# Moving the projection of a turn to the end of its odd unit, with three filler matmuls after each even unit, in a decode attention kernel bound by its loads

## The chip, the cores and the metric

One NeuronCore of a Trainium2 chip runs the whole kernel. The metric is device time in microseconds; the text quotes medians of several executions. The profile's span is about 2 us shorter than the device time of the same execution (443.6 against 445.62 in the profiled run of before), so I compare spans with spans and times with times. Ratios are the mean time of one kernel's runs over the mean of the other's in the same rounds, so they are not quite the ratio of the medians that stand beside them.

## The reference

Two attention layers, A and B, for one new token each, with batch 4, 32 query heads, 8 key/value heads, head size 128; B attends to the last 2048 of 8192 positions only:

```python
q = (x @ wq).reshape(B, 1, 32, 128).transpose(0, 2, 1, 3)
k = repeat(k_cache, 4, axis=1); v = repeat(v_cache, 4, axis=1)   # B: [:, :, Sk - W:, :], W = 2048
p = softmax(einsum("bhqd,bhkd->bhqk", q, k) * 128 ** -0.5)
o = einsum("bhqk,bhkd->bhqd", p, v)
out = o.transpose(0, 2, 1, 3).reshape(B, 1, 32 * 128) @ wo       # A and B concatenated
```

Nearly all of the bytes are the caches, bf16: 184.56 MB are read in all.

## The kernel before

The work is cut into 20 units, 0 to 19: four of B and sixteen of A. One unit is 4 MB of K and 4 MB of V (128 tiles each). Two units make a turn, and TensorE's program is one loop over ten turns, so every turn has the same instructions in the same order. In unit `u` TensorE transposes K tiles (T), multiplies them with the queries (S), sums the weights of the unit before (SM), and multiplies the weights of the unit before with its V (PV):

```python
LA = 3
for k in range(NJ + LA):               # NJ = 16
    if k < NJ:
        TOK.append(("T", k))
    elif k == NJ:
        TOK.append(("SM",))
    else:
        TOK.append(("PV", pc))
        pc += 1
    if k >= LA:
        TOK.append(("S", k - LA))
while pc < NC:                         # NC = 8
    TOK.append(("PV", pc))
    pc += 1
AFTER = {("S", 2): ("OT",), ("S", 5): ("OL",), ("S", 8): ("OPJ",)}
```

So the last two S of a unit stand behind the first two PV. OPJ is the projection of a piece of heads whose attention is done, eight matmuls of 512 columns. It comes after S 8 of the even unit (the flag in the code that says `odd` is true for even `u`):

```python
def fn(pe):
    for i in range(C):                 # C = 8
        ins = pe.matmul(out=bk[0:Bn, 0:D], lhsT=OL[:, i // REP, i % REP, :], rhs=Wo_sb[:, i // REP, i % REP, :],
                        start=(i == 0), stop=(i == C - 1))
    return ins
op("pe", fn, waits=[("E", ol_idx[tn]), ("wo", tn) if tn in pieces else None, bankfree(idx)], inc=("T", idx))
```

Its weights, Wo, are 1 MB for each of the turns 3 to 9, in one tile without a second buffer. All big loads are issued in one order from one queue. K of unit u may be issued when the T of unit u-2 are done, V of unit u-1 when the PV of unit u-3 are done, and Wo of a turn when the projection of the turn before is done:

```python
for u in range(1, NU + 1):             # NU = 20
    if u < NU:
        kv_load("K", u)
    kv_load("V", u - 1)
    tn = (u + 1) // 2
    if u % 2 == 1 and tn in pieces:
        ... op("sp", dma(Wo_sb, src), waits=[("T", opj_idx[tn - 1])], inc=("wo", tn))
```

After the loop comes a tail outside of it: PV of unit 19, a seed from the sums so far, and the last projection with its own tile Wl (1 MB), which is loaded last. V of unit 19 comes in four pieces.

## Time and profile before

| what | value |
|---|---|
| device time, median of 3 runs | 444.65 us (444.62 to 445.03) |
| span of the profile | 443.6 us |
| read from HBM | 184.56 MB, mean 416 GB/s |
| main DMA queue | 98.0% of 16 engines' span |
| TensorE busy | 81% |

These are rows of the page of the kernel before: the clock granted to TensorE, the busy share of the DMA engines and their rate in 40 slices of the span, then the main queue with its packets, MB and share of 16 engines' time, and one line of the list of waits (who waited for whom: us in total, times, longest).

```profile
PEclk9999999999999799789969995999799889968999
DMA  8999999999999999999999999999999999999992
GB/s 332 429 417 421 419 417 421 421 447 406 445 411 449 431 428 429 440 428 428 425 425 434 425 432 432 440 412 442 431 425 425 434 435 431 427 434 415 437 401 73
...
q1 hardware_dynamic: 13088, 184.56, 98.0%
...
PE KT L258 <- DMA K_sb<-in_A_k_cache_dram: 50.6, 8, 7.9
```

The reader should see that the DMA never rests between the first and the last slice, and that TensorE waits for it. Only the last slice (73 GB/s) has room: about 9 us from the end of the bulk of the loads to the end of the kernel.

That tail begins with K of unit 18. These lines are from the timeline of TensorE; the columns are start, us, engine, line, operation, out<-in, shapes, count, and in brackets the idle time before it and what ended it. KT, OT, SA and SB are output tiles of TensorE; KT also serves for the projection and for the last PV. ACT is ScalarE, which computes the exp of the softmax.

```profile
396.74 3.68 PE L258 MATMUL KT<-identf,K_sb 128*128 128x128 f32 x16 [7.94 <-DMA K_sb<-in_A_k_cache_dram]
...
407.54 1.89 PE L370 MATMUL KT<-Wo_sb,OL 128*4 128x512 bf16 x8
...
416.88 1.95 PE L258 MATMUL KT<-identf,K_sb 128*128 128x128 f32 x16
...
427.74 0.63 PE L307 MATMUL OT<-PT,V_sb 128*128 128x64 bf16 x16
...
429.07 2.96 PE L307 MATMUL OT<-PT,V_sb 128*128 128x64 bf16 x96
433.39 1.98 PE L307 MATMUL KT<-PT,V_sb 128*128 128x64 bf16 x64 [1.36 <-ACT PT L448]
```

Unit 18 starts at 396.74, when its K has landed, with the clock at half (16 transposes in 3.68 us; at 416.88 the same 16 take 1.95). The projection of turn 9 is at 407.54. PV of unit 18 runs from 427.74. Then TensorE stands 1.36 us for the last exp, and the PV of unit 19 starts at 433.39.

The last loads, from the timeline of the issuing queue, and the landing of the 4 MB of V of unit 18 (the last line is from the list of DMA issues for the window around 389 us: count, KB, us from issue to landing):

```profile
366.14 0.38 SPq L549 DMA_DIRECT2D Wo_sb<-in_A_wo_dram  x1
368.81 0.33 SPq L549 DMA_DIRECT2D K_sb<-in_A_k_cache_dram  x1
...
383.89 0.80 SPq L549 DMA_DIRECT2D K_sb<-in_A_k_cache_dram  x2
388.89 0.33 SPq L549 DMA_DIRECT2D V_sb<-in_A_v_cache_dram  x1
...
V_sb<-in_A_v_cache_dram SPq DMA_DIRECT2D x1, 4096.0 KB, 37.0
```

Wo of turn 9 goes ahead of K of unit 18; V of unit 18, issued at 388.89, lands at 388.89 + 37.0 = 425.9. That is only 1.8 us before TensorE comes to use it at 427.74.

### The profile page before, as it was taken

The page shows a single profiled execution, that of the slowest core. Times are in us where ns is not written, and L with a number is a line of the kernel's source. Part 1 is how long each engine was busy: PE and PEld are TensorE (multiplying, and loading weights), DVE is VectorE, ACT ScalarE, POOL GpSimd, SP SyncE. Part 2 cuts the span into 40 slices and gives each one's busy share as a digit, 9 for nine tenths or more (in the row PEclk, how much of TensorE's full clock was granted, in tenths as well). Part 3 has the DMA queues.
Part 4 walks back from the last instruction along what each step waited for, and adds up shares of the span by engine and source line. Part 5 has one row for each costly group of instructions (what it writes and reads, how often), then busy time and mean ns, then how long its engine had stood idle before and what let it go on. Part 6 is the DMA issues. An engine that isn't in the chain of part 4 may idle for free.

```text
span 443.6 us, 15670 instructions
## 1 busy us (share of the span) xinstructions
PE 358.4 (81%) x7282; PEld 335.3 (76%) x7282; DVE 210.0 (47%) x472; ACT 184.8 (42%) x184; POOL 21.4 (5%) x56
## 2 busy tenths in 40 slices
PE   0259898998994899399939975996799399929996
PEld 0248798898894889389938975896789389928995
DVE  0035356565463464256525651574355256515661
ACT  1005374374471437054525542562338054515550
POOL 6100000000000000000000000000000000000000
PEclk9999999999999799789969995999799889968999
DMA  8999999999999999999999999999999999999992
GB/s 332 429 417 421 419 417 421 421 447 406 445 411 449 431 428 429 440 428 428 425 425 434 425 432 432 440 412 442 431 425 425 434 435 431 427 434 415 437 401 73
DMA packets 13191, 184.78 MB, mean 416 GB/s; under 512 B 1348, under 2 KB 2424, under 8 KB 4472
## 3 DMA queue, kind: packets, MB, share of 16 engines
q1 hardware_dynamic: 13088, 184.56, 98.0%
q8 instruction: 8, 0.13, 0.1%
q14 instruction: 7, 0.06, 0.0%
q0 software_dynamic: 64, 0.02, 0.0%
q10 hardware_dynamic: 24, 0.01, 0.0%
HBM read 184.56 MB, written 0.01 MB: 416 GB/s over the span
## 4 chain that ended last, share of the span: by engine, by line
DMA 50%; PE 47%; issue 1%; SPq 1%; DVE 1%; ACT 0%
DMA K_sb<-in_A_k_cache_dram 43%; PE KT L258 27%; DMA K_sb<-in_B_k_cache_dram 7%; PE OT L307 5%; PE SA L291 4%; PE KT L370 4%; PE SB L291 3%; PE KT L307 1%; PE SA L319 1%; SPq L549 1%; PE KT L349 0%; PE KT L331 0%; ACT PT L448 0%; PE SA L673 0%; PE KT L673 0%
## 5 line engine op out<-in xcount | busy, mean ns | idle before, releaser
L258 PE MATMUL KT<-identf,K_sb 128*128 128x128 f32 x1280 | 207.7, 297 | 57.3 <-DMA K_sb<-in_A_k_cache_dram 50.6
L267 ACT ACTIVATE KT_sb<-KT 128x1024 bf16<-128x1024 bf16 x160 | 162.4, 1023 | 145.0 <-PE KT L258 144.7
L258 PEld LDWEIGHTS KT<-identf,K_sb 128*128 128x128 f32 x1280 | 148.9, 150 | 65.4 <-DMA K_sb<-in_A_k_cache_dram 51.8
L266 DVE COPY KT_sb<-KT 128x512 int32<-128x512 int32 x160 | 110.3, 689 | 132.1 <-PE KT L258 130.9
L307 PE MATMUL OT<-PT,V_sb 128*128 128x64 bf16 x2560 | 84.4, 193 | 1.7 <-issue 1.7
L307 PEld LDWEIGHTS OT<-PT,V_sb 128*128 128x128 bf16 x2560 | 78.4, 98 | 1.9 <-issue 1.9
L291 PEld LDWEIGHTS SA<-RQc,KT_sb 128*128 128x128 bf16 x1280 | 56.1, 98 | 3.1 <-ACT KT_sb L267 0.6
L448 ACT ACTIVATE PT<-Dt 128x1024 bf16<-128x1024 f32 (+1 forms) x21 | 21.3, 1016 | 85.6 <-DVE Dt L437 85.6
L291 PE MATMUL SA<-RQc,KT_sb 128*128 128x16 bf16 x1280 | 56.2, 170 | 0.0
L291 PE MATMUL SB<-RQc,KT_sb 128*128 128x16 bf16 x1280 | 55.7, 170 | 0.0
L291 PEld LDWEIGHTS SB<-RQc,KT_sb 128*128 128x128 bf16 x1280 | 51.6, 97 | 1.1
L399 DVE TENSOR_REDUCE M<-SB 128x8 f32<-128x512 f32 (+1 forms) x20 | 13.8, 692 | 43.4 <-PE SB L291 43.4
L420 POOL PARTITION_ALL_REDUCE MB<-M1m x20 | 7.7, 387 | 392.9 <-DVE M1m L413 392.9
L370 PE MATMUL KT<-Wo_sb,OL 128*4 128x512 bf16 x80 | 18.9, 379 | 0.0
L189 PE MATMUL KT<-ident,x_sb 4*128 4x4 bf16 x8 | 0.6, 170 | 19.3 <-POOL identf L511 19.3
L189 PEld LDWEIGHTS KT<-ident,x_sb 4*128 4x128 bf16 x8 | 0.4, 112 | 19.5 <-issue 19.5
L437 DVE TENSOR_TENSOR Dt<-SA,MBm 128x512 f32<-128x512 f32 x20 | 13.8, 691 | 0.7
L399 DVE TENSOR_REDUCE M<-SA 128x8 f32<-128x512 f32 (+1 forms) x20 | 13.6, 680 | 0.0
L437 DVE TENSOR_TENSOR Dt<-SB,MBm 128x512 f32<-128x512 f32 x20 | 13.6, 680 | 0.0
L319 PE MATMUL SA<-PT,onesb 128*128 128x64 bf16 x336 | 13.2, 192 | 0.0
L370 PEld LDWEIGHTS KT<-Wo_sb,OL 128*4 128x4 bf16 x80 | 6.0, 84 | 8.1
L319 PEld LDWEIGHTS SA<-PT,onesb 128*128 128x128 bf16 x336 | 11.1, 97 | 0.0
(68 smaller groups left out, 111.8 us busy)
## 6 DMA issues: line engine op xcount, KB each, us to landing
K_sb<-in_A_k_cache_dram SPq DMA_DIRECT2D x15, 4096.0 KB, 27.9
V_sb<-in_A_v_cache_dram SPq DMA_DIRECT2D x15, 4096.0 KB, 32.6
K_sb<-in_B_k_cache_dram SPq DMA_DIRECT2D x16, 1024.0 KB, 21.7
V_sb<-in_B_v_cache_dram SPq DMA_DIRECT2D x16, 1024.0 KB, 21.6
V_sb<-in_B_wq_dram SPq DMA_DIRECT2D x1, 4096.0 KB, 12.3
V_sb<-in_A_wq_dram SPq DMA_DIRECT2D x1, 4096.0 KB, 21.6
Wo_sb<-in_B_wo_dram SPq DMA_DIRECT2D x4, 1024.0 KB, 20.1
K_sb<-in_A_k_cache_dram SPq DMA_DIRECT2D x2, 2048.0 KB, 29.7
```

The source lines that it names most:

```text
L258: ins = pe.transpose(out=bkf[:, pi * 128:(pi + 1) * 128], in_=K_sbf[:, slot, t0:t0 + 2, :].rearrange("p t d -> p (t d)"), identity=identf[ ...
L266: return e.tensor_copy(out=KT_sb.bitcast(I32)[:, tj % NKT, :], in_=bkf.bitcast(I32)[:, :])
L267: return e.activation(out=KT_sb[:, tj % NKT, :], in_=bk[:, :], func=ACTF.Copy)
L291: ins = pe.matmul(out=stb[:, t % NTH * C:(t % NTH + 2) * C], lhsT=ktv[:, pi, :, e], rhs=RQc[:, u % 2, t // TS, e, :], start=(e == 0), stop ...
L307: ins = pe.matmul(out=otb[:, s * NW:s * NW + w], lhsT=V_sb[:, slot, t, :], rhs=PT[:, slot, t * C:t * C + w], start=(j == 0), stop=(j == n ...
L319: ins = pe.matmul(out=SA[u % 2][:, s * NW:(s + 1) * NW], lhsT=onesb[:, :], rhs=PT[:, u % 2, c0:c0 + NW], start=(i == 0), stop=(i == n - 1))
L370: ins = pe.matmul(out=bk[0:Bn, 0:D], lhsT=OL[:, i // REP, i % REP, :], rhs=Wo_sb[:, i // REP, i % REP, :], start=(i == 0), stop=(i == C - 1))
L399: return dve.tensor_reduce(out=M1[:, h * n:(h + 1) * n].rearrange("p (s h) -> p s h", h=C), in_=bank[:, :].rearrange("p (s j h) -> p s h j ...
L420: return pool.partition_all_reduce(MB[:, 0:n], M1m[:, 0:n], channels=128, reduce_op=ReduceOp.max)
L437: return dve.tensor_tensor(out=Dt[:, h * NTH * C:(h + 1) * NTH * C].rearrange("p (s j h) -> p s j h", s=Sh, h=C), in0=bank[:, :].rearrange ...
L448: return act.activation(out=PT[:, u % 2, a:b], in_=Dt[:, a:b], func=ACTF.Exp, scale=scale)
L549: return e.dma_start(out=dst, in_=src)
```

## The change

The intent is to put the projection where TensorE waits anyway (before K of the next even unit), and to fill some of the wait after even units so that TensorE's clock stays up. The core of the diff:

```diff
+        def pe_filler(n):
+            bank = (jobs[-1]["bank"] + 1) % NBK
+            ...
+                for _ in range(n):
+                    ins = pe.matmul(out=KTB[bank][:, :], lhsT=ident[:, :], rhs=RQ[0]..., start=True, stop=True)   # 512 columns, nobody reads it
...
-        AFTER = {("S", 2): ("OT",), ("S", 5): ("OL",), ("S", 8): ("OPJ",)}
+        AFTER = {("S", 2): ("OT",), ("S", 5): ("OL",)}
...
+            if u % 2 == 1:
+                ev["opj"] = pe_job_OPJ(tn)          # after the last PV of the odd unit
+            else:
+                pe_filler(NFILL)                    # NFILL = 3, after the last PV of the even unit
...
-                op("pe", pe_seed)
+                op("pe", pe_seed, waits=[("ocp", NTURN - 1)])
...
-            tn = (u + 1) // 2
-            if u % 2 == 1 and tn in pieces:
+            tn = u // 2
+            if u % 2 == 0 and tn in pieces:
```

The last four lines change the order of the loads. Before: ..., Wo of turn 9, K18, V17, K19, V18. After: ..., K18, V17, Wo of turn 9, K19, V18. This has to be so, because Wo must wait for the projection before it, which is now later.

More of the change, by code (lines that the diff above doesn't have):

```diff
@@ L52, in bass_concat_heads__gqa_block_cached__sliding_block_cached__decode_kernel @@
     NBK = 4
+    NFILL = 3
     NTH = NT // 2
@@ L244, in pe_job_perm, with fn @@
             add(dict(eng="dve", fn=efn, waits=[("T", idx)], inc=("E", idx)))
+        def pe_filler(n):
+            bank = (jobs[-1]["bank"] + 1) % NBK
+            p = bank_last[bank]
+            def fn(pe):
+                ins = None
+                for _ in range(n):
+                    ins = pe.matmul(out=KTB[bank][:, :], lhsT=ident[:, :], rhs=RQ[0][:, :, :, :, :].rearrange("p b g e c -> p (b g e c)"),
+                                    start=True, stop=True)
+                return ins
+            op("pe", fn, waits=[("F", p) if jobs[p]["turn"] is not None else None])
         def pe_T(u, k):
@@ L607, in bass_concat_heads__gqa_block_cached__sliding_block_cached__decode_kernel @@
                     kind = AFTER[tok][0]
-                    anchored({"OT": pe_job_OT, "OL": pe_job_OL, "OPJ": pe_job_OPJ}[kind](tn))
+                    anchored({"OT": pe_job_OT, "OL": pe_job_OL}[kind](tn))
+            if u % 2 == 1:
+                ev["opj"] = pe_job_OPJ(tn)
+            else:
+                pe_filler(NFILL)
+                if tn:
+                    follow[opj_idx[tn - 1]] = tjob_idx[(u, 0)]
             for k in range(0, NJ, 2):
@@ L617, in bass_concat_heads__gqa_block_cached__sliding_block_cached__decode_kernel @@
                     add(d)
-                    if "opj" in d:
-                        follow[d["opj"]] = tjob_idx[(u, k + 2)]
             add(dve_max(u, 1))
@@ L631, in bass_concat_heads__gqa_block_cached__sliding_block_cached__decode_kernel @@
                 add_norm(u - 1)
+            if u % 2 == 1:
+                add(ev["opj"])
             for k in range(1, NJ, 2):
@@ L834, in emit_pe @@
                         else:
-                            assert val <= 0, (we, val)
+                            assert val <= 0 or we[0] == "F", (we, val)
                         o["w"].append((sem, val))
```

## The prediction

> **What bounds it now.** The loads. The page's DMA row is at 9 in 38 of 40 slices; the main queue is 98.0% busy, about 426 GB/s in mid-run. The Trainium skill ("DMA: Bandwidth & Descriptors", Specifications) gives a fabric ceiling of 435 GB/s; the trace agrees that little is left. TensorE follows: in the list of waits it stands 50.6 us for A's K tiles in 8 waits, nearly all just before even units (up to 7.9 us). The queue never runs dry. So only the end can get shorter: K of unit 18 releases TensorE at 396.74, and from there the chain of waits is nearly unbroken TensorE work (units 18 and 19, last softmax, PV, projection) to 443.6.
>
> **What the change does.**
> - Projection (8 matmuls, 1.82 us, in the timeline): leaves the middle of the even unit, where it delays the T and S that follow, and goes to the end of the odd unit, into the wait for the next even K.
> - Fillers: 3 matmuls of 512 columns, at 1.82/8 = 0.23 us each: 0.68 us per turn, off the chain except the set after unit 18.
> - To my mind the largest term: the 1 MB Wo load of a turn moves from before K of the even unit to after it. Every even K from unit 6 on lands 1 MB earlier, about 2.4 us (in the sum of bytes Wo9 takes 380.75 to 383.24). Odd K keeps its position; it is issued later (behind the wait for the projection), but now lands about 30 us after issue; the queue should keep over 10 us of work.
> - TensorE's wait of 7 us per turn is divided: about 2 to 3 us before even units, the rest before odd ones. Clock: it halves after waits of 7 us, and the first 16 transposes take 3.68 us instead of 1.97. The Trainium skill ("TensorE: Matmul & The Clock Gate", Part 1) puts the drop after one idle window of about 3.4 us; here the clock fell 2.5 to 4.7 us after work stopped, agreeing roughly. Shorter waits should keep most even units warm; odd units may now start cold.
>
> **On the critical path.** At the end: K18 2.4 us earlier, projection of turn 9 out of unit 18 −1.8, fillers +0.7, projection at the end of unit 19 +0.3 to +1 (it mostly fits in the 1.36 us in which TensorE waits for exp), warm unit 18 up to −2.5 (partly lost waiting for V18). TensorE could be 3 us or more earlier. But the DMA doesn't end earlier: the last V pieces land near 435.6 and the last Wl piece near 438.4; then follow one pair of matmuls, the copy and the output's transfer (2.6 us from last matmul to end). Floor about 441.4 for the span, a gain of 2.2 us.
>
> **Time:** 442.4 us (−0.5%), range 441.0 to 443.9. Faster by over 2%: 0.02; within 2%: 0.96; slower: 0.02.
>
> **What would show it.** DMA share and GB/s per slice as before; even units' waits down from 7 to under 3.5 us, odd units' up from 0.4 to 3 to 5; fewer half-clock stretches before even units; TensorE waits for VL or Wl pieces in the last 10 us; unit 18 starting near 394.3.
>
> **What would make it wrong.** The later issue of odd K draining the queue (slower); fill or projection delaying T through bank waits; the tail's DMA stragglers moving with the earlier issue of the last V (faster, to 440); even K's landing set by the slowest DMA engine, not by its place in the bytes (no gain).

## More of the kernel before

A trace is that of one execution, and executions of one kernel differ: the spans of the kernel before go from 442.1 to 444.2 us, with a mean of 443.2.

## The result, and the profile after

| | before | changed |
|---|---|---|
| median of 4 runs | 444.79 us (444.62 to 445.03) | 445.9 us (445.18 to 447.0) |
| ratio | | 1.0027, 95% interval 1.0004 to 1.0049 |
| span of the profile | 443.6 us | 444.2 us |

The change makes the kernel slower by 0.3%. It is small, but the sign is clear, and it is not the gain of 2.2 us that I had forecast. The page of the changed kernel, the same rows and waits as above:

```profile
PEclk9999999999989997997999699979998998899989
DMA  8999999999999999999999999999999999999991
GB/s 346 414 415 423 418 418 420 422 446 405 443 437 440 425 426 434 431 425 428 434 428 434 432 437 412 442 425 428 430 437 431 437 425 426 431 420 425 432 404 57
...
q1 hardware_dynamic: 13088, 184.56, 97.9%
...
PE KT L271 <- DMA K_sb<-in_A_k_cache_dram: 42.3, 13, 6.4
PE OT L320 <- DMA V_sb<-in_A_v_cache_dram: 3.5, 1, 3.5
```

The loads run as before. TensorE waits less for K (42.3 instead of 50.6 us, spread over 13 waits instead of 8). There is one new wait, 3.5 us for V, and it happens once. The timeline of TensorE shows where:

```profile
394.47 2.10 PE L271 MATMUL KT<-identf,K_sb 128*128 128x128 f32 x16 [0.32 <-DMA K_sb<-in_A_k_cache_dram]
...
411.72 1.97 PE L271 MATMUL KT<-identf,K_sb 128*128 128x128 f32 x16 [0.69 <-DMA K_sb<-in_A_k_cache_dram]
...
426.32 0.64 PE L320 MATMUL OT<-PT,V_sb 128*128 128x64 bf16 x16 [3.47 <-DMA V_sb<-in_A_v_cache_dram]
...
427.67 4.51 PE L320 MATMUL OT<-PT,V_sb 128*128 128x64 bf16 x96
432.11 1.89 PE L383 MATMUL KT<-Wo_sb,OL 128*4 128x512 bf16 x8
433.93 1.99 PE L320 MATMUL KT<-PT,V_sb 128*128 128x64 bf16 x64
```

And the last loads:

```profile
394.18 0.38 SPq L562 DMA_DIRECT2D Wo_sb<-in_A_wo_dram  x1
394.66 0.89 SPq L562 DMA_DIRECT2D K_sb<-in_A_k_cache_dram  x2
395.65 16.52 SPq L562 DMA_DIRECT2D V_sb<-in_A_v_cache_dram  x5
...
V_sb<-in_A_v_cache_dram SPq DMA_DIRECT2D x1, 4096.0 KB, 30.6
```

The first half of the plan works. Unit 18 starts 2.3 us earlier (394.47 against 396.74), with a full clock (16 transposes in 2.10 us) and without the projection. TensorE is ready for PV of unit 18 at 426.32 - 3.47 = 422.85, against 427.74 before: 4.9 us earlier. But V of unit 18 is issued at 395.65 and lands at 395.65 + 30.6 = 426.3, where it landed before (425.9). Its place in the queue is the same, so the earlier issue brings nothing: in all twelve traces of this document in which the same bytes stand ahead of it, V18 is issued between 388.9 and 395.7 and lands between 425.8 and 426.4.

One thing more stands in the traces. A load is complete when all 16 DMA engines have done their share, and the recorded completions show that 15 of them had done theirs of V18 by 423.2 us in both kernels. The last one followed at 425.9 before and at 426.3 in the changed kernel. So 2.7 to 3.0 us of the landing time belong to one late engine; without it, the wait of the changed kernel would be about 0.4 us (an estimate from these figures: 423.2 less 422.85). Why it is late was not tested.

A ledger of the start of the last PV (433.39 before, 433.93 after):

| step | us |
|---|---|
| ready for PV of unit 18 earlier (427.74 to 422.85) | -4.89 |
| new wait for V18 | +3.47 |
| PV of unit 18 slower (4.29 us from 427.74 to 432.03 before, 5.79 us from 426.32 to 432.11 after) | +1.50 |
| projection now behind it, +1.82, while the wait of 1.36 for exp goes | +0.46 |
| sum | +0.54 |

The slower PV is the clock: 96 matmuls take 4.51 us instead of 2.96. The record of the granted clock has a stretch of half speed from 427.7 to 431.2 us, so it fell 1.4 us after the work had resumed. Without this row the sum would be -0.96 us: the wait takes most of the gain, and the slow clock turns the rest into a loss. The span grew by 0.6 us, so the trace is accounted for. The medians differ by 1.1 us, and the interval of the ratio goes from 0.2 to 2.2 us, so the rest is within the spread of the runs.

### The profile page after: what moved, and what is told of

It reads as the page before. It is cut to its first block, busy times and chain, and to the rows that moved or that the text cites. A ratio compares the mean times of both kernels' runs of the same rounds, so it can differ in the third digit from the quotient of the medians.

```text
span 444.2 us, 15710 instructions
## 1 busy us (share of the span) xinstructions
PE 367.5 (83%) x7312; PEld 339.1 (76%) x7312; DVE 211.0 (48%) x472; ACT 186.3 (42%) x184; POOL 21.3 (5%) x56
## 3 DMA queue, kind: packets, MB, share of 16 engines
q1 hardware_dynamic: 13088, 184.56, 97.9%
HBM read 184.56 MB, written 0.01 MB: 416 GB/s over the span
## 4 chain that ended last, share of the span: by engine, by line
DMA 50%; PE 47%; SPq 1%; issue 1%; DVE 0%; ACT 0%
DMA K_sb<-in_A_k_cache_dram 36%; PE KT L271 23%; PE OT L320 10%; DMA K_sb<-in_B_k_cache_dram 7%; DMA V_sb<-in_A_v_cache_dram 7%; PE KT L383 4%; PE SA L304 4%; PE SB L304 4%; SPq L562 1%; PE SA L332 1%; PE KT L320 1%; PE KT L254 0%; PE SA L692 0%; PE KT L692 0%; DVE oacc L393 0%
## 5 line engine op out<-in xcount | busy, mean ns | idle before, releaser
L271 PE MATMUL KT<-identf,K_sb 128*128 128x128 f32 x1280 | 209.4, 298 | 46.8 <-DMA K_sb<-in_A_k_cache_dram 42.3
L320 PE MATMUL OT<-PT,V_sb 128*128 128x64 bf16 x2560 | 86.0, 194 | 5.1 <-DMA V_sb<-in_A_v_cache_dram 3.5
L320 PEld LDWEIGHTS OT<-PT,V_sb 128*128 128x128 bf16 x2560 | 79.9, 99 | 5.3 <-DMA V_sb<-in_A_v_cache_dram 3.6
L304 PEld LDWEIGHTS SA<-RQc,KT_sb 128*128 128x128 bf16 x1280 | 57.0, 98 | 2.4
```

The costliest lines, as they stand in the source:

```text
L271: ins = pe.transpose(out=bkf[:, pi * 128:(pi + 1) * 128], in_=K_sbf[:, slot, t0:t0 + 2, :].rearrange("p t d -> p (t d)"), identity=identf[ ...
L304: ins = pe.matmul(out=stb[:, t % NTH * C:(t % NTH + 2) * C], lhsT=ktv[:, pi, :, e], rhs=RQc[:, u % 2, t // TS, e, :], start=(e == 0), stop ...
L320: ins = pe.matmul(out=otb[:, s * NW:s * NW + w], lhsT=V_sb[:, slot, t, :], rhs=PT[:, slot, t * C:t * C + w], start=(j == 0), stop=(j == n ...
```

## The experiments

Theory T: at the end TensorE meets the landing of V18, which is fixed by the bytes ahead of it in the queue. All gains ahead of that point are lost there, and what still stands behind it (PV at whatever clock, then the projection) sets the end. "Fixed" covers the late engine as well. Rival F: the fillers' own time ate the gain. Rival Q: the wait for the projection in the load queue delays the issue of odd K and V and so slows the loads. Each run below was compared with the kernel before in the same rounds. The fragments of the timeline are of TensorE, as above, all from the last 20 us.

| run | median us (6 runs) | before, same rounds (11 runs) | ratio, 95% interval | span of profile |
|---|---|---|---|---|
| changed, without fillers | 445.54 | 444.86 | 1.0019 (1.0000 to 1.0038) | 443.6 |
| changed, projection before the PV | 443.64 | 444.86 | 0.9975 (0.9958 to 0.9992) | 441.8 |
| before, with Wo after K | 444.02 | 444.86 | 0.9991 (0.9970 to 1.0011) | 441.9 |
| before, with fillers | 445.71 | 444.86 | 1.0014 (0.9998 to 1.0029) | 444.3 |
| changed, last Wo after V18 | 443.48 | 445.31 | 0.9959 (0.9945 to 0.9972) | 441.4 |
| changed, fillers in the wait for V | 444.04 | 445.31 | 0.9971 (0.9957 to 0.9984) | 442.3 |
| projection before the PV and all S first | 443.51 | 445.31 | 0.9956 (0.9943 to 0.9969) | 442.1 |
| the same, Wl loaded before the last V | 448.47 | 445.31 | 1.0071 (1.0053 to 1.0090) | 445.6 |
| changed, again | 446.21 | 445.08 | 1.0027 (1.0007 to 1.0047) | 444.4 |
| changed, Wo loads at their old place | 444.56 | 445.08 | 0.9991 (0.9973 to 1.0009) | 442.6 |
| before, Wo after K and all S first | 443.58 | 445.08 | 0.9977 (0.9955 to 0.9999) | 441.7 |

### The fillers: taken out of the changed kernel, and added alone

```diff
-                pe_filler(NFILL)          # in the changed kernel
```

> The changed kernel without its fillers (odd-end projection and late Wo kept). Theory T (at the end TensorE stands for V of unit 18, which lands near 426.3 whatever TensorE does, and what still stands behind that wait in TensorE's order sets the end): no gain over the changed kernel, within 0.5 us of its 445.9; TensorE only stands longer for V18, some 4.2 us instead of 3.5. Rival F (the fillers' own time is what ate the gain): at least 0.7 us faster than the changed kernel. Rival Q (the later issue of odd K and V slows the loads): no change.

```profile
411.24 1.97 PE L271 MATMUL KT<-identf,K_sb 128*128 128x128 f32 x16 [1.27 <-DMA K_sb<-in_A_k_cache_dram]
...
425.84 0.64 PE L320 MATMUL OT<-PT,V_sb 128*128 128x64 bf16 x16 [3.46 <-DMA V_sb<-in_A_v_cache_dram]
...
427.37 4.24 PE L320 MATMUL OT<-PT,V_sb 128*128 128x64 bf16 x96
```

445.54 us: no clear gain over the changed kernel. The wait for V18 did not grow to 4.2 us as expected. The time of the fillers went into the wait for K of unit 19 instead, which is 1.27 us here and 0.69 us with the fillers, so TensorE comes to V18 no earlier in relation to the loads (K of unit 19 and V18 both landed 0.5 us earlier in this run). The half clock is still there.

```diff
+        def pe_filler(n):
+            ...
+            if u % 2 == 0:
+                pe_filler(NFILL)          # in the kernel before, after the even unit
```

> The kernel before with only the three fillers after each even unit. Theory T: there TensorE reaches PV of unit 18 after V18 has landed (427.7 against 425.9), so the set after unit 18 lies on the chain: +0.7 us, 445.5; elsewhere hidden in waits. Rival F: +0.7 us or more, up to 7 us if each turn's set counted. Rival Q: nothing to say.

```profile
428.41 0.63 PE L320 MATMUL OT<-PT,V_sb 128*128 128x64 bf16 x16
```

445.71 us, with the interval of the ratio reaching just below 1. In the trace PV of unit 18 starts 0.67 us later than before (427.74), which is one set of fillers. So the nine other sets of fillers are hidden in waits, and the set after unit 18 counts in the kernel before, where TensorE neither waits for K of unit 19 nor for V18. It doesn't count in the changed kernel, where TensorE waits for both. Rival F explains the second run but not the first.

### The projection moved a little: before the PV instead of after it

```diff
+                if u % 2 == 1 and tok == ("S", NJ - 3):
+                    ev["opj"] = pe_job_OPJ(tn)
...
-            if u % 2 == 1:
-                ev["opj"] = pe_job_OPJ(tn)
-            else:
+            if u % 2 == 0:
                 pe_filler(NFILL)
```

> The changed kernel with the projection of the odd unit put just before the first PV of that unit instead of after the last. Theory T: in the last turn it fits into the wait for V18, which shrinks from 3.5 to about 1.7 us; the first PV of the last unit starts at 431 to 432 instead of 433.9; 1.8 to 3.3 us faster than the changed kernel (the upper end if the clock stays full), so 442.6 to 444. Rival F: no change against the changed kernel. Rival Q: the issue of odd K comes 6 us earlier, so the bytes of the whole queue would end earlier than 437.1; under T they end where they did.

```profile
422.73 1.89 PE L383 MATMUL KT<-Wo_sb,OL 128*4 128x512 bf16 x8
425.89 0.64 PE L320 MATMUL OT<-PT,V_sb 128*128 128x64 bf16 x16 [1.27 <-DMA V_sb<-in_A_v_cache_dram]
...
427.24 2.96 PE L320 MATMUL OT<-PT,V_sb 128*128 128x64 bf16 x96
431.53 1.98 PE L320 MATMUL KT<-PT,V_sb 128*128 128x64 bf16 x64 [1.33 <-ACT PT L461]
```

443.64 us, as theory T expects, and faster than before with an interval clear of 1. The projection lies in the wait, the wait shrinks to 1.27 us, the clock stays full (2.96 us), and the last PV starts at 431.53. The last packet of Wl in the trace ends at 438.0 us here, at 438.4 in the changed kernel, and at 438.0 in the kernel before (the 437.1 in the expectation is not an end of the loads in the trace). So the earlier issue of odd K that comes with this edit did not move the loads' end by more than these 0.4 us, and rival Q has little to explain.

### V18 moved: one load of 1 MB put behind it

```diff
-            tn = u // 2
-            if u % 2 == 0 and tn in pieces:
+            tn = 9 if u == 19 else u // 2
+            if (u % 2 == 0 and u < 18 or u == 19) and tn in pieces:
```

> The changed kernel with one load of 1 MB elsewhere: the last Wo is loaded after V of unit 18 instead of before K of unit 19. Fillers and the projection at the end of the odd unit stay. Theory T: V18 lands 2.4 us earlier (near 423.9), the wait before the PV of unit 18 shrinks from 3.5 to 1 to 2 us, too short to lower the clock; PV and projection then end near 430, and the last PV starts at 430 to 431 instead of 433.9: span 441.5 to 442.3, about 2 us faster than the changed kernel. If V18 is not the cause (rivals F, Q): no change, 445 to 446.

```profile
423.16 0.67 PE L320 MATMUL OT<-PT,V_sb 128*128 128x64 bf16 x16 [1.95 <-DMA V_sb<-in_A_v_cache_dram]
...
424.95 3.89 PE L320 MATMUL OT<-PT,V_sb 128*128 128x64 bf16 x96
428.78 1.89 PE L383 MATMUL KT<-Wo_sb,OL 128*4 128x512 bf16 x8
430.61 1.99 PE L320 MATMUL KT<-PT,V_sb 128*128 128x64 bf16 x64
...
436.65 0.27 PE L692 MATMUL SA<-Wl_sb,OT_sb 128*4 128x256 bf16 x1 [0.36 <-DMA Wl_sb<-in_A_wo_dram]
```

This is the most direct test: TensorE's program is untouched, with its fillers and its projection at the end; only the place of one load among the last ones differs. PV of unit 18 starts at 423.16 instead of 426.32, and the kernel takes 443.48 us. So the place of the last loads is the cause. The edit brings K of unit 19 1 MB forward too, and TensorE comes to V18 1.64 us earlier for that (421.21 instead of 422.85); with V18 where it was, this would only have made the wait longer. One detail of my expectation was wrong: the half clock did come (96 matmuls in 3.89 us, half speed from 423.6 to 427.0), after a wait of only 1.95 us. It cost nothing at the end: the first piece of the last V, issued at 409.88, landed 20.7 us later at 430.6, and the last PV starts at 430.61. After that TensorE runs along with the end of the loads: in the last line it is a piece of Wl that ends its wait.

### The clock: fillers in the wait for V

```diff
+                if u % 2 == 1 and tok == ("S", NJ - 3):
+                    pe_filler(14)
```

> The changed kernel with 14 more fillers (3.2 us) in every odd unit just before its first PV, so TensorE works while it would stand for V18. Theory T with the clock as a part of it: the half clock at 427.7 goes, the last 96 matmuls of PV take 2.96 us again instead of 4.51, the last PV starts 1.5 us earlier: about 1.5 us faster than the changed kernel, still with the projection on the chain: about 444.4. If the clock plays no part: no change or slower. Rival F: slower by the fillers' time.

```profile
425.97 0.64 PE L320 MATMUL OT<-PT,V_sb 128*128 128x64 bf16 x16 [0.43 <-DMA V_sb<-in_A_v_cache_dram]
...
427.32 2.96 PE L320 MATMUL OT<-PT,V_sb 128*128 128x64 bf16 x96
430.21 1.89 PE L383 MATMUL KT<-Wo_sb,OL 128*4 128x512 bf16 x8
432.03 1.99 PE L320 MATMUL KT<-PT,V_sb 128*128 128x64 bf16 x64
```

444.04 us. Adding 3.2 us of useless work to every odd unit makes the changed kernel faster. The 96 matmuls are back at 2.96 us (1.55 us less), and the last PV starts 1.90 us earlier than in the changed kernel; the other 0.35 us is V18 landing at 425.97 instead of 426.32 in this run. So the half clock is worth 1.5 us, more than the whole loss: without it the changed kernel is faster than before (0.9971). The fillers of the change itself stand after the even unit, where no such wait is on the chain.

### The two halves of the change, one at a time

First the load order alone, in the kernel before:

```diff
         if u < NU:
             kv_load("K", u)
-        kv_load("V", u - 1)
-        tn = (u + 1) // 2
-        if u % 2 == 1 and tn in pieces:
+        tn = u // 2
+        if u % 2 == 0 and tn in pieces:
             ...                            # load Wo of turn tn
+        kv_load("V", u - 1)
```

> The kernel before with one thing of the change: Wo of a turn is loaded after K of its even unit instead of before. Theory T: K of unit 18 lands about 2.4 us earlier (394.3), TensorE reaches the PV of unit 18 at about 425.3 and stands under 1.5 us for V18 (426); no projection follows, so the last PV starts at about 431 instead of 433.4: 1.5 to 2.4 us faster than before, 442.4 to 443.3. Rival F: the full 2.4 us. Rival Q: the same as T. If even K is not earlier, my account of the order of bytes is wrong: 444.8.

```profile
426.05 0.64 PE L307 MATMUL OT<-PT,V_sb 128*128 128x64 bf16 x16 [0.84 <-DMA V_sb<-in_A_v_cache_dram]
...
431.69 1.98 PE L307 MATMUL KT<-PT,V_sb 128*128 128x64 bf16 x64 [1.33 <-ACT PT L448]
```

In the trace it is as expected: unit 18 starts at 394.27, the wait for V18 is 0.84 us, the last PV starts at 431.69 instead of 433.39, the span is 441.9. In time it is a miss: the median of 444.02 is above my range, and the ratio 0.9991 is not clear of 1. Two of its six runs were at 445.4 and 445.9, with a lower mean clock (0.946 and 0.942, against 0.950 to 0.961 in the others). Their traces were not kept; that a half clock fell into the tail in them is likely, but not shown.

Then the projection alone, with the Wo loads where they were. This gives a wrong result, since the loads go to spare tiles:

```diff
+        Wx = [sb("Wx%d" % i, [128, 2, REP, D], BF16) for i in range(2)]
...
-            tn = u // 2
-            if u % 2 == 0 and tn in pieces:
+            tn = (u + 1) // 2
+            if u % 2 == 1 and tn in pieces:
-                ... dma(Wo_sb, src), waits=[("T", opj_idx[tn - 1])]
+                ... dma(Wx[tn % 2], src), waits=[("T", opj_idx[tn - 2])]
```

> The changed kernel (projection at the end of the odd unit, fillers) with the Wo loads' place in the queue as in the kernel before. That place is only free of races if the loads go to two spare tiles that nobody reads, so the result is wrong on purpose; bytes and instructions are the same, and the issue of odd K and V no longer stands behind the projection. Theory T: even K lands where it did (unit 18 from 396.7), TensorE reaches the PV of unit 18 near 426.6, after V18: no wait above 0.5 us, no half clock in the tail; PV then projection end near 432.6, the last PV from there: 0.4 to 0.9 us faster than before, thus about 1.5 us faster than the changed kernel. Each half of the change alone gains then, and only together they lose. If the projection's place alone is the loss, it is slower than before here too (445.5 or more).

```profile
426.33 0.63 PE L321 MATMUL OT<-PT,V_sb 128*128 128x64 bf16 x16
...
427.67 2.96 PE L321 MATMUL OT<-PT,V_sb 128*128 128x64 bf16 x96
430.56 1.89 PE L384 MATMUL KT<-Wo_sb,OL 128*4 128x512 bf16 x8
432.38 1.99 PE L321 MATMUL KT<-PT,V_sb 128*128 128x64 bf16 x64
```

444.56 us (444.31 to 445.07), where the changed kernel in the same batch took 446.21 (445.60 to 446.99), so the runs don't overlap. TensorE arrives just as V18 has landed, and the clock is full. Against the kernel before it is 1.0 us better in the trace (432.38 against 433.39), and not clear of it in time. By its one trace each half gains, in time neither is clear of the kernel before; together they lose. They are not independent, because the second half brings TensorE to V18 earlier than V18 can be there, and what comes of that is a wait and a half clock. This run undoes the wait in the load queue too, so by itself it doesn't separate Q from T; the run with one load moved does.

### The changed kernel again

> The changed kernel once more, unedited, for more runs beside the kernel before on the chip of the other runs of this batch. 1.001 to 1.004 of before; V18 waited for 3 to 4 us, the last PV from about 433.9.

446.21 us, 1.0027 of before, the same as the first time. In its trace the wait for V18 is 3.46 us and the last PV starts at 434.11.

### Can more be had? All S first, and Wl earlier

In addition to the projection before the PV, all S of an odd unit go before its first PV, so that the last softmax no longer waits for V18:

```diff
+        TOK_ODD = [t for t in TOK if t[0] != "PV"] + [t for t in TOK if t[0] == "PV"]
...
-            for tok in TOK:
+            for tok in (TOK_ODD if u % 2 == 1 else TOK):
```

> The run with the projection before the odd unit's PV, with in addition all S matmuls of an odd unit before its first PV, so that the last softmax does not wait for V18. Theory T: exp of unit 19 is ready before PV of unit 18 is done, the 1.33 us wait for it goes, the last PV starts near 430.2; then the DMA decides (last V pieces near 435.5, last Wl piece near 438.4): span 441.2 to 441.8, so 0 to 0.6 us faster than 443.64. More than that would say that the DMA's end is not the floor.

```profile
426.45 3.91 PE L320 MATMUL OT<-PT,V_sb 128*128 128x64 bf16 x128 [1.16 <-DMA V_sb<-in_A_v_cache_dram]
431.72 1.98 PE L320 MATMUL KT<-PT,V_sb 128*128 128x64 bf16 x64 [1.36 <-DMA V_sb<-in_A_v_cache_dram]
```

443.51 us. The wait of 1.33 us for exp is gone, and one of 1.36 us for the first piece of the last V has taken its place. So the loads are the floor, as I had expected, but it bites earlier: I had put the last PV near 430.2 and the span at 441.8 or less, against 431.72 and 442.1 in this trace. Whether this is any faster than the run with the projection alone before the PV (443.64, in another batch), the runs don't tell. The same two edits on the kernel before (Wo after K, all S first, no fillers, projection where it was) are within its expected range too:

> The kernel before with Wo loaded after K of the even unit and all S matmuls of the odd unit before its first PV; no fillers, projection where it was. Theory T: TensorE reaches PV of unit 18 near 425.3, waits under 1 us, exp of unit 19 is ready in time, the last PV starts at 430.2 to 431, then the DMA's end is the floor: span 441.3 to 442, 443.2 to 443.8 where before is at 445.0.

443.58 us, ratio 0.9977 with an interval that ends at 0.9999; two of its six runs were at 444.9 and 445.2. The lowest spans of the four quickest variants lie within 0.3 us: 441.3 (this one), 441.4 (all S first), 441.4 (one load moved), 441.6 (projection before the PV). My forecast floor was 441.4.

Loading Wl ahead of the last V was a miss:

> As the run with all S first, with Wl loaded before the last V instead of after it. The bytes are the same. The last V piece (512 KB) then lands last, near 438; after it 16 PV matmuls, the norm, 16 projection matmuls and the output, about 5.5 us: if the DMA's end is the floor, 442 to 444, not faster than with Wl last. If the slow end of the DMA (rate falling from 434 us on) belongs to the small rows of Wl, it could be 1 to 2 us faster.

```profile
434.01 3.27 PE L320 MATMUL KT<-PT,V_sb 128*128 128x64 bf16 x64 [3.98 <-DMA V_sb<-in_A_v_cache_dram]
```

448.47 us, 0.7% slower than before, worse than I had allowed for. I had counted only the work after the last piece of V. But Wl now stands ahead of all of V19, its first piece of 2 MB lands at 434.0, TensorE waits 3.98 us, the clock falls (64 matmuls in 3.27 us instead of 1.98), and the whole PV of unit 19 is behind that.

## Why the prediction was wrong, point by point

- "The loads" bind, the rate doesn't change, and the queue doesn't run dry: right. 97.9% busy, 184.56 MB, the last packet of the loads ends at 438.4 against 438.0 us.
- Even K lands 2.4 us earlier because Wo goes behind it: right. 394.47 against 396.74.
- Shorter waits before even units and longer before odd ones: right in kind, off in size. In the changed kernel the timeline of the A units up to 18 shows waits of 1.11 us or less before the even ones (I had said 2 to 3), and of 5.40 to 6.44 before the odd ones from 7 to 17 (I had said the rest of the 7 us). Those odd units start at half clock: 16 transposes take 3.37 to 3.68 us, against 2.10 in the even ones.
- "TensorE could be 3 us or more earlier": right up to V18, by 4.9 us, and nothing after it. In it, "fillers +0.7" was no cost in the changed kernel: they lie in the wait for K of unit 19.
- "partly lost waiting for V18", put only against the gain of a warm unit 18: this is the step that failed. The wait took 3.47 of all the 4.89 us gained. I summed gains on TensorE across a point where a load of fixed landing time stood, without writing that time down. The page and the trace gave it: 388.89 + 37.0 = 425.9, only 1.8 us of margin in the kernel before. With it the sum is a maximum: whatever is gained before 425.9, at most 1.8 us of it gets through. The wait for V18 was 3.47 us.
- "projection at the end of unit 19 +0.3 to +1": right. It stands behind V18 and costs its 1.82 us there, of which the 1.36 us of the exp wait come back: +0.46.
- Not in the sum at all, and the second part of the failed step: the clock falls from the wait for V18 and makes PV 1.5 us slower. I had thought of the clock for the starts of units, and not for the tail.
- The floor of 441.4 us by the end of the loads: the quickest executions of the runs that remove these terms have spans of 441.3 to 441.6. The traces with all S first wait for a piece of the last V, the one with a load moved for a piece of Wl; the one with the projection before the PV (441.8) still waits 1.33 us for exp. So the size was right; the changed kernel just doesn't come near it.
- "What would make it wrong" named the queue running dry, bank waits, moving stragglers, and even K's landing set by the slowest engine. None of these was the cause. K of unit 18 did land with one engine 2.7 us (before) and 3.0 us (changed) behind the others, as V18 did, but it still came 2.3 us earlier.

With the wait at 3.47 us, the clock's 1.50 us put in, and the projection's 0.46 us, against 4.89 us gained, the sum is +0.54 us, as the ledger shows, and the span grew by 0.6.

## What to carry to other kernels

In a kernel bound by its loads, write down the landing times of the last few loads beside the times at which they are used. A gain ahead of such a landing passes only up to the margin, and work that is moved behind it is paid in full. So move off-chain work to just before a wait on the chain rather than just after it, and check in the trace whether the wait you create lowers TensorE's clock: its length alone doesn't tell (it fell after 1.95 us with one load moved, and stayed full after 2.74 us, 371.08 to 373.82, in the kernel before with Wo after K and all S first). If TensorE can't be moved, a small load that is not urgent can be: putting 1 MB behind V18 instead of before it turned a loss of 0.3% into a gain of 0.4%.

## What the Trainium skill lacked or had wrong

- "TensorE: Matmul & The Clock Gate", Part 1, gives one idle window of about 3.4 us before the clock falls to half. Here it fell after a wait of only 1.95 us (one load moved: idle until 423.16, half clock from 423.6), so a window need not be wholly idle; after a wait of 1.27 us it did not fall.
- The same page, Part 4, says that transposes don't count as busy for the full clock. In the kernel before, 16 f32 transposes alone (from 187.57, 3.55 us) ran at half clock, and the granted clock was full again from 190.86, before any other matmul ran (the next is at 190.96). (The kernel makes them with `pe.transpose`; the trace calls them MATMUL and doesn't show the mode.) The table of stretches shows it, in the column before DMA share and GB/s:

```profile
185.00:190.00 5.00, 2.43 (x12) 2.43 (x13) 0.69 (x1) 0.42 (x1) 0.00 (x0) 0.50 0.99 426
190.00:195.00 5.00, 5.00 (x75) 4.75 (x73) 2.78 (x6) 3.36 (x4) 0.00 (x0) 0.91 0.97 419
```

- "DMA: Bandwidth & Descriptors", Specifications, lists a limit of about 358 GB/s from HBM for one NeuronCore, half of a stack's 716 GB/s. This kernel, which uses one core only, read 416 GB/s over its whole span, so the row is no limit for a core that reads alone. The page's fabric ceiling of 435 GB/s agrees with the 425 to 435 GB/s of most of the later slices (single slices show up to 449).
- The same page, in the section on why a DMA adds 16 to its semaphore, says that the 16 engines finish independently, without a size for it. In the changed kernel fifteen engines had landed their share of V18 by 423.2 us and the last one at 426.3. The wait for V18 was almost all a wait for one engine.
